# A two-pass attention backward kernel: first-pass steps re-ordered, one PSUM bank per head's softmax, slots for long VectorE work, output product per head

## Chip, cores, metric

One core of one Trainium2 chip. The metric is the device time of one execution in microseconds, as the median of several. Kernels that are compared ran on the same chip in alternating rounds; a ratio is the mean time of one kernel's fast runs over the mean of the other's fast runs of the same rounds, so it is not quite the ratio of the medians quoted beside it. A run over 1.5% above the fastest of its kernel counts as slow and stays out of the ratios. A verdict is "faster" or "slower" when the whole 95% interval of the ratio lies beyond 2%, "same" when it lies within 2%, and "unclear" when it reaches across that bound.

In the profile lines PE is TensorE (its matmuls), PEld its weight loads, DVE is VectorE, ACT ScalarE, POOL GpSimd, SP SyncE. The granted clock (PEclk) is the share of TensorE's full clock that the profile records. Stage figures come from the one profiled run of each kernel.

## The reference, cut to what matters

A transformer block in decode form (one query token, batch 2) and all its gradients:

```python
B, Sq, D = 2, 1, 640;  Hq = Hkv = 32;  Sk, Dh = 4096, 128;  Dff = 1728      # bf16
h  = x + softmax((LN(x) @ wq) . k_cache * Dh**-0.5) . v_cache @ wo
h2 = h + relu(LN(h) @ w1) @ w2
# outputs: h2 and the gradients of x, k_cache, v_cache, wq, wo, w1, w2 for a given grad_out
```

There are 64 (batch, head) pairs, each with 1 MB of K and 1 MB of V. K and V are read once in a first pass (scores, softmax, output and some sums), V once more in a second pass, and 2 MB of gradients are written per pair. The kernel moves 372.7 MB in all.

## The kernel before: the parts that matter

The first pass is a software pipeline over i: stage c works on head i (transposes of K, scores), p on head i-1 (softmax, P times K), r on head i-2 (sums over V). One generator yields after each step. In the iterations read in the timelines (kernel before, 77 to 85 us) PE and VectorE keep the order in which this code issues their instructions, apart from PE's weight loads, which run ahead of matmuls.

```python
def p1_iter(i, dve_group):
    ...
    # step 0: KT0 = transpose_group(K, 0)                       PE, copied out by ScalarE
    # step 1: u_half(0), KT1, mx_ps <- rmax, gmax, m_part(0)
    # step 2: scores 0, KT2, nb, ep = exp(...), u_half(1), m_part(1)
    # step 3: scores 1, KT3, m_part(2), pk_part(0)
    # step 4: scores 2, m_part(3), tot_ps, pk_part(1)
    # step 5: m_part(4), m_part(5); VectorE: tot, rtot, P_bf, pk_part(2)
    if c is not None:                                         # step 6
        matvec_group(c["s"], c.pop("KT3"), 3, q)
        rmax = small.tile([128, 1], BF16, tag="rmax", name="rmax")
        nc.vector.reduce_max(out=rmax[:], in_=c["s"][:], axis=AX.X)
        c["rmax"] = rmax
    if r is not None:
        m_part(6)
    if p is not None:
        pk_part(3)
    yield
    # step 7: m_part(7), MT and OU written by ScalarE
```

The attention output of all heads goes through wo in the middle of the run, after the first batch:

```python
def middle_gen(b):
    nc.vector.tensor_copy(out=OFc[:, :, b], in_=OU[:, b, :, 0])
    yield
    a_ps = pst([128, ND], FP32, "mid", "a_ps")
    for c in range(ND):
        for h in range(H):
            nc.tensor.matmul(a_ps[:, c:c + 1], lhsT=wo_t[:, h, c * 128:(c + 1) * 128], rhs=OFc[:, h, b:b + 1], ...)
            if h % (4 if b == 0 else 8) == 3:
                yield
    # norm, MLP forward and backward, then go_group: what the second pass needs
```

`middle_gen` is background work: a few of its yields run per step, by a credit (`RATES`). The second pass starts at i = 49, every second iteration, and runs alone from i = 66 on. The kernel divides PSUM (the memory that its matmuls write) into eight banks by tag, `PSB`; the tag "tiny" is one bank that all small softmax results shared.

## Time and profile before

| | before |
|---|---|
| median of 3 | 1045.98 us (1043.9 to 1046.0) |
| span of the profiled run | 1044.0 us |
| HBM traffic | 372.7 MB, mean 357 GB/s |
| heads 12, 31, 43, 46, 63 leave the first pass at | 116.3, 246.4, 338.8, 364.6, 530.4 us |

The clock hands of the last row are the copies MT, one per head, at the end of its first pass. From the profile's page, the busy share of PE and DMA and the granted clock in tenths, in 40 slices of 26.1 us:

```profile
PE   6999989999998988878895665547998987676795
PEclk9988999899969889887875575566555555667555
DMA  9999999999857578898999999999899998999697
```

To see: PE and DMA both near 90% in the first ten slices, DMA low in slices 11 to 15 (the middle), and PE near half clock in the second pass (0.59 and 0.57 in the two windows from 530 to 960 us), where DMA is full (0.98 and 0.97).

### The profile page before, as it was taken

What the parts mean: (1) busy time and instruction counts of PE and PEld (TensorE: products, weight loads), DVE (VectorE), ACT (ScalarE), POOL (GpSimd) and SP (SyncE); (2) the same over time, 40 slices, a digit from 0 to 9 for tenths busy, and PEclk for the clock granted to TensorE, in tenths of its full rate; (3) what the DMA queues carried; (4) which work ended last, traced back from release to release, by engine and by line L of the source; (5) the groups of instructions that cost most, each with busy time, mean ns of one, the idle gap of its engine ahead of it and who ended that gap; (6) DMA issues with size and microseconds to landing.
All of it is one profiled execution on the core that took longest, in us unless ns stands there. A gap on an engine that the chain in (4) does not pass through costs nothing.

```text
span 1044.0 us, 32292 instructions
## 1 busy us (share of the span) xinstructions
PE 843.8 (81%) x14111; PEld 730.7 (70%) x14111; DVE 698.8 (67%) x1654; ACT 644.8 (62%) x985; POOL 95.2 (9%) x216
## 2 busy tenths in 40 slices
PE   6999989999998988878895665547998987676795
PEld 5988888889987887778784554436675765665553
DVE  3656777766549777776665768777876755566465
ACT  4555555467766586667674564546777766555684
POOL 0000000000000000000011111111111111111121
PEclk9988999899969889887875575566555555667555
DMA  9999999999857578898999999999899998999697
GB/s 350 382 400 405 363 364 379 347 349 351 323 206 282 205 278 314 346 379 342 363 413 425 371 384 394 355 402 361 326 412 422 398 393 329 421 422 401 231 374 319
DMA packets 59758, 372.70 MB, mean 357 GB/s; under 512 B 5760, under 2 KB 15424, under 8 KB 17376
## 3 DMA queue, kind: packets, MB, share of 16 engines
q1 hardware_dynamic: 38960, 221.50, 56.2%
q0 software_dynamic: 20656, 149.14, 34.7%
q8 instruction: 110, 1.80, 0.7%
q14 instruction: 32, 0.26, 0.1%
HBM read 221.48 MB, written 149.13 MB: 355 GB/s over the span
## 4 chain that ended last, share of the span: by engine, by line
PE 40%; DMA 26%; DVE 16%; issue 10%; ACT 5%; POOL 1%; SPq 0%; POOLq 0%; ACTq 0%; DVEq 0%
PE t_ps L274 16%; DMA out_dram<-gV 15%; PE m_ps L304 9%; DMA Wt<-in_A_v_cache_dram 6%; DVE pk L310 5%; DVE gK L550 4%; PE o_ps L652 4%; PE m_ps L320 4%; PE s_ps L285 3%; DVE junk L436 3%; ACT t_sb L279 2%; DMA Vt<-in_A_v_cache_dram 2%; DMA Kt<-in_A_k_cache_dram 2%; PE dp_ps L285 1%; DVE gV L550 1%
## 5 line engine op out<-in xcount | busy, mean ns | idle before, releaser
L279 ACT COPY t_sb<-t_ps 128x1024 bf16<-128x1024 bf16 x489 | 490.4, 1013 | 190.4 <-PE t_ps L274 184.1
L274 PE MATMUL t_ps<-ident_bf,Wt 128*128 128x128 bf16 x2048 | 239.2, 289 | 16.6 <-DMA Wt<-in_A_v_cache_dram 15.3
L274 PEld LDWEIGHTS <-Wt 128*128 128x128 bf16 x2048 | 185.4, 132 | 67.7 <-issue 50.0
L285 PEld LDWEIGHTS <-t_sb 128*128 128x128 bf16 x4096 | 171.1, 104 | 67.4 <-ACT t_sb L279 58.5
L310 DVE TENSOR_TENSOR pk<-Kt,ep 128x1024 bf16<-128x1024 bf16 x256 | 174.5, 683 | 45.0 <-ACT ep L353 41.2
L550 DVE TENSOR_TENSOR gV<-rb,pp 128x2048 bf16<-128x2048 bf16 x128 | 155.8, 1217 | 66.8 <-DMA out_dram<-gK 31.7
L550 DVE TENSOR_TENSOR gK<-rb,gsp 128x2048 bf16<-128x2048 bf16 x128 | 153.6, 1218 | 59.5 <-DMA out_dram<-gV 59.5
L304 PE MATMUL m_ps<-pk,Vt 128*128 128x129 bf16 x2048 | 193.3, 234 | 0.0
L274 PE MATMUL t_ps<-ident_bf,Kt 128*128 128x128 bf16 x2048 | 172.9, 234 | 2.3 <-DMA Kt<-in_A_k_cache_dram 2.3
L304 PEld LDWEIGHTS <-Vt 128*128 128x128 bf16 x2048 | 135.8, 104 | 4.5
L274 PEld LDWEIGHTS <-Kt 128*128 128x128 bf16 x2048 | 132.4, 104 | 3.6 <-DMA Kt<-in_A_k_cache_dram 2.7
L285 PE MATMUL dp_ps<-goc,t_sb 128*128 128x1 bf16 x2048 | 97.6, 169 | 45.7 <-ACT t_sb L279 43.4
L594 POOL DMA_DIRECT2D out_dram<-gV x64 | 34.2, 534 | 667.7 <-DVE gV L550 638.1
L285 PE MATMUL s_ps<-qc,t_sb 128*128 128x1 bf16 x2048 | 89.3, 164 | 4.2 <-DVE gsp L585 2.0
L406 ACT ACTIVATE MT<-m_ps,rtot 128x128 bf16<-128x128 f32 x64 | 23.5, 368 | 105.3 <-PE m_ps L304 105.3
L320 PEld LDWEIGHTS <-Kt 128*128 128x128 bf16 x2048 | 64.7, 97 | 20.3 <-issue 18.9
L277 DVE COPY t_sb<-t_ps 128x1024 bf16<-128x1024 bf16 x43 | 29.7, 690 | 71.6 <-PE t_ps L274 71.5
L320 PE MATMUL m_ps<-ep,Kt 128*128 128x1 bf16 x2048 | 70.8, 164 | 7.6 <-ACT OU L407 6.3
L655 ACT CAST ot<-o_ps 128x512 bf16<-128x512 f32 (+3 forms) x120 | 59.8, 526 | 11.7 <-PE o_ps L652 10.4
L564 ACT CAST rb<-rb_ps 128x256 bf16<-128x256 f32 x64 | 24.4, 381 | 49.7 <-DVE gK L550 37.9
L610 POOL DMA_DIRECT2D out_dram<-gK x64 | 34.0, 531 | 226.8 <-DVE gK L550 183.7
L436 DVE CUSTOM_DVE_ANT_0 junk<-wo_t,hbc 128x640 bf16<-128x640 bf16 x64 | 52.1, 815 | 0.1
(168 smaller groups left out, 703.2 us busy)
## 6 DMA issues: line engine op xcount, KB each, us to landing
Kt<-in_A_k_cache_dram SPq DMA_DIRECT2D x64, 1024.0 KB, 8.0
Vt<-in_A_v_cache_dram SPq DMA_DIRECT2D x64, 1024.0 KB, 7.6
Wt<-in_A_v_cache_dram SPq DMA_DIRECT2D x64, 1024.0 KB, 10.6
out_dram<-gV POOLq DMA_DIRECT2D x64, 1024.0 KB, 8.2
out_dram<-gK POOLq DMA_DIRECT2D x64, 1024.0 KB, 9.3
wo_t<-in_A_wo_dram SPq DMA_DIRECT2D x4, 1280.0 KB, 9.5
wqs<-in_A_wq_dram SPq DMA_DIRECT2D x5, 1024.0 KB, 17.4
out_dram<-ot POOLq DMA_DIRECT2D x5, 1024.0 KB, 5.5
```

What stands on the lines that cost most here:

```text
L274: nc.tensor.transpose(t_ps[:, j, :], nat[:, g * GT + j, :], ident_bf[:])
L279: nc.scalar.copy(out=t_sb[:], in_=t_ps[:])
L285: nc.tensor.matmul(dst[:, sc:sc + 1], lhsT=t_sb[:, j, :], rhs=vec, start=True, stop=True)
L304: nc.tensor.matmul(r["m"][:, 0:129], lhsT=r["V"][:, sc, :], rhs=r["pk"][sc // GT][:, sc % GT, 0:129], start=False, stop=(sc == NSC - 1))
L310: nc.vector.tensor_tensor(out=pk[:, :, 0:128].rearrange("p s (a two) -> p s a two", two=2), in0=p["K"][:, sl, :].rearrange("p s (a two) -> ...
L320: nc.tensor.matmul(r["m"][:, 129:130], lhsT=r["K"][:, sc, :], rhs=r["ep"][:, sc, 0:1], start=(sc == 0), stop=False)
L436: nc.vector.tensor_tensor_reduce(out=junk[0:kc, 0:width], in0=in0, in1=in1, scale=1.0, scalar=0.0, op0=ALU.mult, op1=ALU.add, accum_out=acc)
L550: nc.vector.tensor_tensor(out=pairs_view(dst[:, sl, :]), in0=row.rearrange("p (a two) -> p a two", two=2)[:, None, :, :].to_broadcast([128 ...
L594: nc.gpsimd.dma_start(out=natural(out_3, b, h), in_=gV[:])
L610: nc.gpsimd.dma_start(out=natural(out_2, bp, hp), in_=gK[:])
L652: nc.tensor.matmul(o_ps[0:P, 0:nn], lhsT=L[:, bass.ds(c0 + k, P, step=cc)], rhs=R[:, n0:n0 + nn], start=True, stop=True)
L655: nc.scalar.copy(out=ot[0:P, k, n0:n0 + nn], in_=o_ps[0:P, 0:nn])
```

## The change

Its intent, as far as the code shows it: let nothing in the first pass wait for the shared scratch bank; put long VectorE reductions only where no engine waits behind them; take the two bursts of 160 wo products out of the middle, so that the second pass can begin three iterations earlier; spread the second pass's steps over the iteration, and load its V tile (W) one iteration earlier. The core of the diff (cuts marked):

```diff
-    PSB = {"tps": 2, "sps": 3, "m": 1, "tiny": 1, "mid": 1}
+    PSB = {"tps": 2, "sps": 3, "m": 1, "a": 1, "mid": 1}
@@ p1_iter: steps 0 to 4 re-ordered (KT0, KT1 together; both u halves together; nb, ep at step 3) ... @@
+            c["bank"] = pst([128, 512], FP32, "sps", "s_ps")     # mx, nb, tot in other columns of it
@@ step 5 @@
         if r is not None:
-            m_part(4)
             m_part(5)
+        if c is not None:
+            matvec_group(c["s"], c.pop("KT3"), 3, q)
+            rmax = small.tile([128, 1], BF16, tag="rmax", name="rmax")
+            nc.vector.reduce_max(out=rmax[:], in_=c["s"], axis=AX.X)
+            c["rmax"] = rmax
         if p is not None:
+            pk_part(2)
             tot = ...; rtot = ...; P_bf[...] = ...
-            pk_part(2)
@@ new @@
+    def a_head():
+        b, h = pairs[a_next[0]]
+        if h == 0:
+            a_bank[0] = pst([128, ND], FP32, "a", "a_ps")
+        nc.vector.tensor_copy(out=OFc[:, h, b:b + 1], in_=OU[:, b, h, 0:1])
+        for c in range(ND):
+            nc.tensor.matmul(a_bank[0][:, c:c + 1], lhsT=wo_t[:, h, ...], rhs=OFc[:, h, b:b + 1], ...)
+        a_next[0] += 1
+    def a_heads(i): ...            # up to two heads g <= i - 3
@@ slots @@
+    def turn():
+        while slot[0] <= 0:
+            yield 0.0
+        slot[0] -= 1
@@ go_group, gx2 and ga reductions @@
+            yield from turn()
@@ second pass: dp and row broadcasts in one bank, gK first, then transposes, gV last; 7 background
@@ steps per second-pass head where there were 5; steps placed by MIXED and REST in the mixed stage
-    M0_ITERS = 15
+    M0_ITERS = 12
+        ahead = plan[n + 1][1] if n + 1 < len(plan) and ii is not None else jj    # W queued earlier
@@ main loop @@
+        for k, _ in enumerate(p1_iter(i, i < H + 1)):
+            ...
+            if k == 5:
+                a_heads(i)
+            pump()
+            slot[0] = ...          # 1 or 2 at k = 1, 1 at k = 6, else 0
+            bg_step(0, rate)
```

Not shown: the weights are loaded in another order (the pieces of wo before w1), the credit of the background work is capped, MT has 50 buffers instead of 52, and the weight gradients' outputs rotate over three banks instead of two.

More of the change, by code (lines that the diff above doesn't have):

```diff
@@ L54 @@
     GH = 8
-    NMT = 52
+    NMT = 50
     def f_kc(c):
@@ L326, in p1_iter @@
             c["KT0"] = transpose_group(c["K"], 0)
+            c["KT1"] = transpose_group(c["K"], 1)
         yield
@@ L330, in p1_iter @@
             u_half(0)
-        if c is not None:
-            c["KT1"] = transpose_group(c["K"], 1)
+            u_half(1)
+            give(r["Kg"])
         if p is not None:
@@ L335, in p1_iter @@
             bhp = bp * H + hp
-            mx_ps = pst([1, 128], FP32, "tiny", "mx_ps")
-            nc.tensor.matmul(mx_ps[:], lhsT=p["rmax"][:], rhs=ident_bf[:], start=True, stop=True)
+            mx = p["bank"][0:1, 64:192]
+            nc.tensor.matmul(mx, lhsT=p["rmax"][:], rhs=ident_bf[:], start=True, stop=True)
             gmax = small.tile([1, 1], BF16, tag="gmax", name="gmax")
-            nc.vector.reduce_max(out=gmax[:], in_=mx_ps[:], axis=AX.X)
+            nc.vector.reduce_max(out=gmax[:], in_=mx, axis=AX.X)
         if r is not None:
@@ L343, in p1_iter @@
         if c is not None:
-            c["s"] = pst([128, NSC], FP32, "sps", "s_ps")
+            c["bank"] = pst([128, 512], FP32, "sps", "s_ps")
+            c["s"] = c["bank"][:, 0:NSC]
             matvec_group(c["s"], c.pop("KT0"), 0, q)
             c["KT2"] = transpose_group(c["K"], 2)
+        if r is not None:
+            m_part(1)
+        yield
+        if c is not None:
+            matvec_group(c["s"], c.pop("KT1"), 1, q)
         if p is not None:
-            nb_ps = pst([128, 1], FP32, "tiny", "nb_ps")
-            nc.tensor.matmul(nb_ps[:], lhsT=ones_bf[0:1, :], rhs=gmax[:], start=True, stop=True)
+            nbp = p["bank"][:, 200:201]
+            nc.tensor.matmul(nbp, lhsT=ones_bf[0:1, :], rhs=gmax[:], start=True, stop=True)
             nb = small.tile([128, 1], FP32, tag="nb", name="nb")
-            nc.scalar.mul(out=nb[:], in_=nb_ps[:], mul=-SCALE)
+            nc.scalar.mul(out=nb[:], in_=nbp, mul=-SCALE)
             ep = small.tile([128, NSC, 2], BF16, tag="ep", name="ep")
@@ L356, in p1_iter @@
         if r is not None:
-            u_half(1)
-            give(r["Kg"])
-            m_part(1)
+            m_part(2)
+        if c is not None:
+            c["KT3"] = transpose_group(c["K"], 3, dve_group)
         yield
-        if c is not None:
-            matvec_group(c["s"], c.pop("KT1"), 1, q)
-            c["KT3"] = transpose_group(c["K"], 3, dve_group)
-        if r is not None:
-            m_part(2)
         if p is not None:
             pk_part(0)
-        yield
+            pk_part(1)
+        if r is not None:
+            m_part(3)
         if c is not None:
@@ L371, in p1_iter @@
         if r is not None:
-            m_part(3)
+            m_part(4)
         if p is not None:
-            tot_ps = pst([128, NSC], FP32, "tiny", "tot_ps")
-            nc.tensor.matmul(tot_ps[:], lhsT=ones_bf[:], rhs=ep[:, :, 0], start=True, stop=True)
-            pk_part(1)
+            totp = p["bank"][:, 256:256 + NSC]
+            nc.tensor.matmul(totp, lhsT=ones_bf[:], rhs=ep[:, :, 0], start=True, stop=True)
         yield
         if r is not None:
-            m_part(4)
             m_part(5)
+        if c is not None:
+            matvec_group(c["s"], c.pop("KT3"), 3, q)
+            rmax = small.tile([128, 1], BF16, tag="rmax", name="rmax")
+            nc.vector.reduce_max(out=rmax[:], in_=c["s"], axis=AX.X)
+            c["rmax"] = rmax
         if p is not None:
+            pk_part(2)
             tot = small.tile([128, 1], FP32, tag="tot", name="tot")
-            nc.vector.reduce_sum(out=tot[:], in_=tot_ps[:], axis=AX.X)
+            nc.vector.reduce_sum(out=tot[:], in_=totp, axis=AX.X)
             rtot = small.tile([128, 1], FP32, tag="rtot", name="rtot")
@@ L388, in p1_iter @@
             p["rtot"] = rtot
-            pk_part(2)
         yield
-        if c is not None:
-            matvec_group(c["s"], c.pop("KT3"), 3, q)
-            rmax = small.tile([128, 1], BF16, tag="rmax", name="rmax")
-            nc.vector.reduce_max(out=rmax[:], in_=c["s"][:], axis=AX.X)
-            c["rmax"] = rmax
         if r is not None:
@@ L410, in p1_iter, with a_heads @@
         yield
+    a_next = [0]
+    a_bank = [None]
+    def a_head():
[4 more added lines that the diff above has]
+        for c in range(ND):
+            nc.tensor.matmul(a_bank[0][:, c:c + 1], lhsT=wo_t[:, h, c * 128:(c + 1) * 128], rhs=OFc[:, h, b:b + 1],
+                             start=(h == 0 and c == 0), stop=(h == H - 1 and c == ND - 1))
+        a_next[0] += 1
+    def a_heads(i):
+        for _ in range(2):
+            g = a_next[0]
+            if g > i - 3 or g >= NP1:
+                return
+            b, h = pairs[g]
+            if b == 0 and i < W_AT[1 + h * 4 // H] + 4 or b > 0 and ("a", b - 1) not in done:
+                return
+            a_head()
     def bcast_cols(colsrc, n, kc_of, dst):
@@ L437, in ttr @@
                                        op0=ALU.mult, op1=ALU.add, accum_out=acc)
+    slot = [99]
+    def turn():
+        while slot[0] <= 0:
+            yield 0.0
+        slot[0] -= 1
     def one(src, b):
@@ L467, in middle_gen @@
     def middle_gen(b):
-        nc.vector.tensor_copy(out=OFc[:, :, b], in_=OU[:, b, :, 0])
-        yield
-        a_ps = pst([128, ND], FP32, "mid", "a_ps")
-        for c in range(ND):
-            for h in range(H):
-                nc.tensor.matmul(a_ps[:, c:c + 1], lhsT=wo_t[:, h, c * 128:(c + 1) * 128], rhs=OFc[:, h, b:b + 1],
-                                 start=(h == 0), stop=(h == H - 1))
-                if h % (4 if b == 0 else 8) == 3:
-                    yield
+        while a_next[0] < (b + 1) * H:
+            a_head()
+            yield
+        a_ps = a_bank[0]
         at_bf = small.tile([128, ND], BF16, tag="at_bf", bufs=1, name="at_bf")
@@ L481, in middle_gen @@
         nc.vector.tensor_copy(out=h32[:, 0, :], in_=h1c[:, :, b])
-        yield
+        yield ("a", b)
         yield from ln_fwd(h32[:], 1, x2c[:, :, b:b + 1], rstd2[:, b:b + 1])
@@ L507, in middle_gen @@
             for k in range(3):
+                yield from turn()
                 ttr(w1_t[:, c, k * FW:(k + 1) * FW], fbc[:, k * FW:(k + 1) * FW], gx2p[:, c, k:k + 1], FW)
@@ L540, in ga_gen @@
                 kc = f_kc(c)
+                yield from turn()
                 ttr(w2_t[0:kc, c, :], gbc[0:kc, :], ga[0:kc, b, c:c + 1], D, kc)
@@ L553, in outer_half @@
             in1=colp[:, sl, None, :].to_broadcast([128, HALF, 64, 2]), op=ALU.mult)
-    def p2_rows(j):
-        b, h = pairs[j]
-        rb_ps = pst([128, 256], FP32, "tiny", "rb_ps")
-        nc.tensor.matmul(rb_ps[:, 0:128], lhsT=goc[:, h, b:b + 1].to_broadcast([128, 128]), rhs=ident_bf[:],
-                         start=True, stop=True)
-        nc.tensor.matmul(rb_ps[:, 128:256], lhsT=qsc[:, h, b:b + 1].to_broadcast([128, 128]), rhs=ident_bf[:],
-                         start=True, stop=True)
-        rb = mats.tile([128, 256], BF16, tag="rb", bufs=3, name="rb")
-        nc.scalar.copy(out=rb[:], in_=rb_ps[:])
-        pp = small.tile([128, NSC, 2], BF16, tag="pp", name="pp")
-        nc.gpsimd.tensor_copy(out=pp[:], in_=P_bf[:, b * H + h, :, None].to_broadcast([128, NSC, 2]))
-        S2.setdefault(j, {}).update(rb=rb, pp=pp)
     def p2_iter(j):
@@ L572, in p2_iter @@
         p = S2[j - 1] if j - 1 in S2 else None
-        if c is not None:
-            b, h = pairs[j]
-            go = goc[:, h, b:b + 1]
-            if "rb" not in c:
-                p2_rows(j)
-            c["T0"] = transpose_group(c["W"], 0)
-            gV = take("g", [128, NSC, 128], "gV")
-            outer_half(gV, c["rb"][:, 0:128], c["pp"], 0)
         if p is not None:
@@ L587, in p2_iter @@
                 in1=P_bf[:, bp * H + hp, :, None].to_broadcast([128, NSC, 2]), op0=ALU.add, op1=ALU.mult)
-        yield
         if c is not None:
-            c["dp"] = pst([128, NSC], FP32, "sps", "dp_ps")
-            c["T1"] = transpose_group(c["W"], 1)
-            matvec_group(c["dp"], c.pop("T0"), 0, go)
-            outer_half(gV, c["rb"][:, 0:128], c["pp"], 1)
-            nc.gpsimd.dma_start(out=natural(out_3, b, h), in_=gV[:])
-            give("g")
-        yield
-        if c is not None:
-            c["T2"] = transpose_group(c["W"], 2)
-            matvec_group(c["dp"], c.pop("T1"), 1, go)
+            b, h = pairs[j]
+            go = goc[:, h, b:b + 1]
+            bank = pst([128, 512], FP32, "sps", "dp_ps")
+            for k, col in enumerate((goc, qsc)):
+                nc.tensor.matmul(bank[:, 128 + k * 128:256 + k * 128],
+                                 lhsT=col[:, h, b:b + 1].to_broadcast([128, 128]), rhs=ident_bf[:],
+                                 start=True, stop=True)
+            c["dp"] = bank[:, 0:NSC]
+            rb = mats.tile([128, 256], BF16, tag="rb", bufs=3, name="rb")
+            nc.scalar.copy(out=rb[:], in_=bank[:, 128:384])
+            pp = small.tile([128, NSC, 2], BF16, tag="pp", name="pp")
+            nc.gpsimd.tensor_copy(out=pp[:], in_=P_bf[:, b * H + h, :, None].to_broadcast([128, NSC, 2]))
+            c.update(rb=rb, pp=pp)
+            c["T0"] = transpose_group(c["W"], 0)
         if p is not None:
@@ L603, in p2_iter @@
         yield
-        if c is not None:
-            c["T3"] = transpose_group(c["W"], 3)
-            give(c["Wg"])
-            matvec_group(c["dp"], c.pop("T2"), 2, go)
         if p is not None:
@@ L613, in p2_iter @@
         yield
-        if j + 1 < NP1 and ("go", (j + 1) // H, ((j + 1) % H) // GH) in done:
-            p2_rows(j + 1)
+        if c is None:
+            return
+        c["T1"] = transpose_group(c["W"], 1)
+        matvec_group(c["dp"], c.pop("T0"), 0, go)
+        yield
+        c["T2"] = transpose_group(c["W"], 2)
+        matvec_group(c["dp"], c.pop("T1"), 1, go)
+        yield
+        c["T3"] = transpose_group(c["W"], 3)
+        give(c["Wg"])
+        matvec_group(c["dp"], c.pop("T2"), 2, go)
+        gV = take("g", [128, NSC, 128], "gV")
+        outer_half(gV, c["rb"][:, 0:128], c["pp"], 0)
+        yield
+        outer_half(gV, c["rb"][:, 0:128], c["pp"], 1)
+        nc.gpsimd.dma_start(out=natural(out_3, b, h), in_=gV[:])
+        give("g")
         yield
@@ L650, in outer_rows @@
                     fw[0] += 1
-                    o_ps = pst([128, 512], FP32, "mid" if fw[0] % 2 else "m", "o_ps")
+                    o_ps = pst([128, 512], FP32, ("mid", "m", "a")[fw[0] % 3], "o_ps")
                     nc.tensor.matmul(o_ps[0:P, 0:nn], lhsT=L[:, bass.ds(c0 + k, P, step=cc)], rhs=R[:, n0:n0 + nn],
@@ L733, in bg_step @@
         q = (bg, bg2)[k]
-        credit[k] = credit[k] + rate if q else 0.0
+        credit[k] = min(credit[k] + rate, 2.0) if q else 0.0
         while q and credit[k] > 0.0:
-            credit[k] -= bg_one(q)
+            took = bg_one(q)
+            credit[k] -= took
+            if took == 0.0:
+                break
     def bg_until(mark):
+        slot[0] = 99
         while mark not in done:
             assert bg_one(bg) > 0.0, mark
-    M0_ITERS = 15
+    M0_ITERS = 12
     P2_AT = H + 2 + M0_ITERS
@@ L764 @@
                 queue.append(("K", ii))
-        if jj is not None and jj < NP1:
-            queue.append(("W", jj))
+        ahead = plan[n + 1][1] if n + 1 < len(plan) and ii is not None else jj
+        if ahead is not None and ahead < NP1 and ("W", ahead) not in queue:
+            queue.append(("W", ahead))
         if ii is not None and 1 <= ii <= NP1:
@@ L769 @@
         if ii in W_AT:
-            queue.append(("w", (5, 4, 0, 1, 2, 3)[W_AT.index(ii)]))
+            queue.append(("w", (5, 0, 1, 2, 3, 4)[W_AT.index(ii)]))
     queue.insert(0, ("wq", 0))
@@ L793, with p2_step @@
     fin = None
-    for n, (i, j) in enumerate(plan):
-        gens = []
-        if i is not None:
-            if i % QP == 0 and 1 <= i // QP < NQ:
-                q_piece(i // QP)
-                pump()
-            gens.append(p1_iter(i, i < H + 1))
+    g2 = None
+    MIXED = {1: 2, 3: 1, 4: 1, 6: 1}
+    REST = {1: 1}
+    def p2_step():
+        nonlocal g2
+        try:
+            next(g2)
+        except StopIteration:
+            g2 = None
+    for n, (i, j) in enumerate(plan):
+        if i is not None and i % QP == 0 and 1 <= i // QP < NQ:
+            q_piece(i // QP)
+            pump()
         if n + 3 < len(plan) and plan[n + 3][1] is not None:
@@ L803 @@
         if j is not None:
+            while g2 is not None:
+                p2_step()
             if j < NP1:
                 bg_until(("go", j // H, (j % H) // GH))
-            gens.append(p2_iter(j))
+            g2 = p2_iter(j)
         if i is None and j >= H - 1:
@@ L814 @@
             bg.append(("ga", ga_gen()))
-        rate = RATES[0 if i is not None and i <= H + 1 else 1 if j is None else 2 if i is not None else
-                     3 if j <= H else 4]
-        while gens:
-            for g in list(gens):
-                try:
-                    next(g)
-                except StopIteration:
-                    gens.remove(g)
-                    continue
+        rate = RATES[0 if i is not None and i <= H + 1 else 1 if j is None and i < P2_AT else
+                     2 if i is not None else 3 if j <= H else 4]
+        if i is None:
+            slot[0] = 99
+            while g2 is not None:
+                p2_step()
                 pump()
@@ L826 @@
                 bg_step(1, RATE2)
+            continue
+        at = MIXED if j is not None else REST
+        for k, _ in enumerate(p1_iter(i, i < H + 1)):
+            for _ in range(at.get(k, 0)):
+                if g2 is not None:
+                    p2_step()
+            if k == 5:
+                a_heads(i)
+            pump()
+            slot[0] = ((2 if rate == RATES[1] else 1) if k == 1 else 1 if k == 6 else 0) if i < P2_AT else int(k == 6)
+            bg_step(0, rate)
+            bg_step(1, RATE2)
         if i is not None and i in (H + 1, NP1 + 1):
```

## The prediction

> **What bounds the kernel now.** I read the page's busy shares and 40 slices first, then one window per stage, then one first-pass iteration in the timeline, then the waits of the mixed stage.
>
> No engine is the bound over the whole run, so the run has to be cut into stages. The scaled softmax rows (MT, one per head, written when a head leaves the first pass) are the clock hands: head 12 leaves at 116.3 us, head 31 at 246.4, head 46 at 364.6, head 63 at 530.4. The windows between them, with columns us, then busy us per engine, granted clock, DMA share and GB/s:
>
> ```profile
> core 0: us, PE busy (x) PEld busy (x) DVE busy (x) ACT busy (x) POOL busy (x), PEclk, DMA share, GB/s
> 116.00:246.00 130.00, 118.67 (x2567) 109.35 (x2565) 97.39 (x321) 75.31 (x136) 0.00 (x0) 0.97 0.96 359
> 246.00:365.00 119.00, 110.55 (x2312) 102.67 (x2310) 79.68 (x290) 79.31 (x131) 0.00 (x0) 0.88 0.74 266
> 365.00:530.00 165.00, 139.62 (x2708) 129.72 (x2706) 119.92 (x316) 113.04 (x172) 11.05 (x24) 0.87 0.88 340
> 530.00:706.00 176.00, 103.14 (x1656) 91.88 (x1653) 121.07 (x186) 92.41 (x114) 27.36 (x62) 0.59 0.98 391
> 706.00:960.00 254.00, 208.29 (x2390) 163.37 (x2391) 168.93 (x258) 173.48 (x257) 42.05 (x94) 0.57 0.97 389
> 960.00:1044.00 84.00, 62.28 (x562) 40.29 (x560) 46.76 (x60) 51.40 (x76) 12.86 (x28) 0.50 0.77 311
> ```
>
> To see: from 530 on the DMA engines are 97 to 98% busy at about 390 GB/s, so the second pass alone is bound by transfers. Up to 246 PE (91% busy) and DMA (96%) run close together. From 246 to 365, where the output projection, norms and MLP are threaded in, DMA falls to 266 GB/s and PE sets the pace. From 365 to 530 (both passes mixed) PE is 85% busy and DMA 88%.
>
> How tight PE is in a smooth first-pass iteration (6.17 us, heads 5 to 9) is seen at the end of one:
>
> ```profile
> 78.23 0.34 PE L285 MATMUL s_ps<-qc,t_sb 128*128 128x1 bf16 x8
> 78.41 0.47 PEld L304 LDWEIGHTS <-Vt 128*128 128x128 bf16 x8
> 78.43 0.63 PE L304 MATMUL m_ps<-pk,Vt 128*128 128x129 bf16 x8
> ```
>
> PE goes from the last score group (78.23) to the next product 0.20 us later. By such start-to-start pitches: transposes 4 x 0.55, score groups 4 x 0.2, column sums 0.8, m products 1.9, three small ones 0.3, together 6.0 us of the 6.17. Thus any wait put on PE's path is added almost whole.
>
> In the mixed stage a pair of iterations (one with, one without a second-pass head) takes 19.8 to 22.2 us by the same hands; the late load of W costs some 2 to 3 us of it:
>
> ```profile
> PE t_ps L274 <- DMA Wt<-in_A_v_cache_dram: 6.3, 3, 2.5
> ```
>
> [...] every iteration keeps the order of the source. So a matmul that waits for VectorE holds all PE work behind it. [...] (clock 0.50 at 290 to 300 us, where the norm's chain stalls PE; 1.00 at 130 to 140 us, where PE was 83% busy with short gaps). [...] here the uses inside the shared bank follow one another by data anyway, so I expect no new wait from that in the first pass.
>
> **Part by part.**
>
> *One bank per head's softmax, both column-sum halves together, transposes 0 and 1 together.* Removes the shared one-buffer scratch bank and small waits at the iteration's head: ScalarE's OU copy (0.16 us), rmax (0.15 to 0.2). K's buffer is released about 0.8 us earlier. Gain about 0.2 us of 6.17: base 6.0. In the mixed stage the three banks rotate over dp, s, s: the next dp always takes the previous dp's bank, so PE must wait for gsp between the last score group and the row broadcast: about 0.35 + 0.28 + 0.1 = 0.75 us per pair, new.
>
> *VectorE slots.* The long multiply-reduces (0.75 to 0.82 us; 28 for `ga`, 23 before the second pass can start) move to where nothing waits. Before, iterations with them ran at 6.6 to 7.4 us (heads 13 to 18) against 6.17. Gain up to 0.7 us each over about 15 iterations, some 8 us, if nothing else takes it.
>
> *wo product per head.* Takes two bursts of 160 products away (PE 16.9 us busy in all; the first, 8 us, lies on PE's path around 250 to 286, the second in the DMA-bound part). But each head's five products are issued at step 5, just after the last score group, and they read OFc, a VectorE copy queued **behind** rmax, pk part 2, tot, rtot and P_bf of the same step. rmax itself needs that score group. Pitches of those on VectorE from the timeline: rmax 0.10, pk 0.61 + 0.07, tot 0.22, rtot 0.19, P_bf 0.15, then the copy about 0.15, plus about 0.15 for the score group's own drain beyond its 0.20 pitch and the semaphores: **1.65 us in which PE waits**, where it now needs no wait at all. In the kernel before the same wait exists once, when a whole OFc is copied:
>
> ```profile
> who waited for it (us, times):
>   PE a_ps L473: 1.4, 1
> ```
>
> That is this wait's size by itself. With the products (5 x 0.045 to 0.05 = 0.25 us) an iteration becomes 6.0 + 1.65 + 0.25 = 7.9 us. It holds from i = 15 (with one exception, i = 19, where no head is due) to i = 65, since heads of the second batch start at i = 35, one per iteration.
>
> *Second pass three iterations earlier (12 for 15), W loaded one iteration earlier, its steps spread.* One more second-pass head lies in the mixed stage: 10 for 9; one fewer in the tail, 8 us. The middle fits: about 27 short steps (3.4 iterations), 15 reduces at three per iteration (5), 1 for the norm backward, 8 more reduces (2.7): 12 to 12.4 iterations.
>
> **The sum** (first-pass index i; head i-2 leaves at its end):
> - to the start of i = 15: 116.3 before, DMA-bound at over 400 GB/s in much of it; after 114.
> - i = 15 to 33: before 130 us. After 18 x 7.9 + 6.0 = 148.
> - i = 34 to 45: after 12 x 7.9 + 8 for the norm's stalls (in the kernel before, heads 38 and 39 took 11.3 each) = 103. Second pass starts at 365; before at 364.6, but then three heads further on.
> - mixed: work per pair 2 x 6.25 + 3.3 (32 transposes 2.2, scores 0.8, rows 0.3) = 15.8, at a clock near 0.9 17.5 us; waits 2 x 1.65 + 0.75 + about 0.5 for ScalarE copies = 4.5; 22 us. DMA would need 7.34 MB at 390 GB/s = 18.8, so PE binds. Ten pairs, the last without loads of K: 217. First pass ends at 582 (before 530).
> - tail: before 514; one head fewer, 8; some 10 from three banks for the weight gradients' outputs (their stretch 960 to 1044 runs at 311 GB/s) and more background steps per head: 496.
> Total 1078 span, about 1080 measured.
>
> **Rivals.**
> *A: the wait is hidden.* If PE would have waited there anyway (for DMA or ScalarE), the 1.65 us vanish. Then first pass to i = 33 in 240, 12 iterations at 6.7 plus 8, mixed pairs at the DMA's 19.3, tail 496: 240 + 88 + 191 + 496 = 1015 to 1030. For it: VectorE is free enough, W's wait goes, DMA sits at 0.74 in the middle. Against: PE's 97% in smooth iterations, and DMA demand at 7.9 us is only about 2.55 MB / 7.9 = 323 GB/s, so no transfer wait covers it. I give 0.25.
> *B: the wait is there in the first pass but the transfers pay it back*: loads run ahead and the DMA-bound tail takes less. The buffers (7 + 3 of 1 MB) hold at most about 10 MB, some 25 us, and they are full in the middle already. It would give 1045 to 1060. I give 0.25.
> *C: the wait is there in full, and the new banks or gsp wait cool PE's clock in the mixed stage*: 1080 to 1095. The full-wait case with C together 0.5.
>
> **Range and chances.** Weighting 1080 (0.5), 1055 (0.25) and 1025 (0.25) gives about 1060 in the mean, with the bulk above; I say 1066, 8 in 10 between 1018 and 1092. Over 2% slower means above 1067: 0.49. Over 2% faster means below 1025: 0.17. Between: 0.34.
>
> **What would show it.** Right: a wait of PE's a_ps products for VectorE's OFc of 1.4 to 1.8 us, about 50 times, 70 to 90 us in all; MT spacing near 7.9 us from head 13 to 43, where DMA share falls to 0.85; head 63 leaving near 580; W's wait gone. Wrong: OFc waits under 0.5 us each, or spacing under 7 us at DMA share over 0.95 (rival A), or a tail shorter than 480 us (B).

Its sum: 114 + 148 + 103 + 217 + 496 = 1078 us. What it says of the clock at 290 to 300 us misreads the trace and is corrected in the point-by-point part.

## The result, and the profile after

The changed kernel takes 1157.42 us in the median (1146.69 to 1164.6, 4 runs, the longest of them slow), before 1045.99 (4 runs, the fourth at 1056.22); the ratio of the fast runs is 1.101 (95% interval 1.0889 to 1.1131). It is 10% slower: the direction of the prediction, outside its range.

The same three lines of the page, slices now of 28.8 us:

```profile
PE   6998887777888788777877675567698976679763
PEclk8999687777777657988787756556555556855555
DMA  9999787756646436898898999899899989959998
```

The first four slices are close to those before. From the fifth on, about i = 15, clock and DMA fall and stay low until the second pass. By stage, from the stage windows of the changed kernel, cut at its own hands (heads 12, 31, 43, 63):

```profile
core 0: us, PE busy (x) PEld busy (x) DVE busy (x) ACT busy (x) POOL busy (x), PEclk, DMA share, GB/s
108.00:297.00 189.00, 147.37 (x2712) 142.95 (x2710) 103.75 (x361) 74.25 (x135) 0.00 (x0) 0.77 0.71 264
297.00:429.00 132.00, 108.88 (x1813) 103.64 (x1811) 68.65 (x255) 63.66 (x106) 0.00 (x0) 0.68 0.51 185
429.00:643.00 214.00, 174.84 (x3276) 165.50 (x3274) 135.21 (x365) 128.10 (x202) 12.72 (x29) 0.82 0.85 319
643.00:1152.00 509.00, 365.19 (x4378) 288.00 (x4374) 340.13 (x512) 315.84 (x441) 91.37 (x179) 0.56 0.93 369
```

Who waited for the tile OFc in the changed kernel (us in all, times):

```profile
  PE a_ps L426: 90.1, 48
```

And one iteration's end in its timeline (start, duration, engine, line; the bracket is the engine's idle time before):

```profile
221.46 0.69 DVE L277 COPY t_sb<-t_ps 128x1024 bf16<-128x1024 bf16 x1 [1.27 <-PE t_ps L274]
222.07 0.68 DVE L310 TENSOR_TENSOR pk<-Kt,ep 128x1024 bf16<-128x1024 bf16 x1
222.21 0.35 PE L285 MATMUL s_ps<-qc,t_sb 128*128 128x1 bf16 x8
222.74 0.69 DVE L310 TENSOR_TENSOR pk<-Kt,ep 128x1024 bf16<-128x1024 bf16 x1
...
223.41 0.19 DVE L387 TENSOR_REDUCE rmax<-s_ps 128x1 bf16<-128x32 f32 x1
223.51 0.69 DVE L310 TENSOR_TENSOR pk<-Kt,ep 128x1024 bf16<-128x1024 bf16 x1
...
224.60 0.24 DVE L395 TENSOR_SCALAR P_bf<-ep,rtot 128x32 bf16<-128x32 bf16 x1
224.75 0.21 DVE L423 CAST OFc<-OU 128x1 bf16<-128x1 f32 x2
...
224.96 0.39 PE L426 MATMUL a_ps<-OFc,wo_t 128*128 128x1 bf16 x10 [2.40 <-DVE OFc L423]
```

To see: PE's last score group ends at 222.56. VectorE is then still at pk parts 0 and 1 of the same head; rmax starts only at 223.41, and OFc comes behind pk part 2, tot, rtot and P_bf. PE stands still for 2.40 us. In the first batch VectorE also copies one of the four transposed groups out of PSUM, just ahead of this (L277, 0.69 us). In the second batch ScalarE makes that copy, and each wait is 1.6 us. That the copy makes the difference fits its length, but was not tested. The waits in heads 31 to 43:

```profile
PE a_ps L426 <- DVE OFc L423: 17.6, 11, 1.6
```

What the wait of 2.40 us does to the clock shows in two windows of its iteration, ahead of the wait's end and behind it:

```profile
218.00:225.00 7.00, 4.60 (x111) 4.39 (x109) 4.49 (x17) 2.67 (x5) 0.00 (x0) 0.94 0.95 377
225.00:230.00 5.00, 5.00 (x87) 4.87 (x87) 1.66 (x5) 2.45 (x4) 0.00 (x0) 0.57 1.02 408
```

After the wait PE is busy all the time, at a granted clock of 0.57. In heads 12 to 31 of this trace the clock records are 1.0 or 0.5 in turn, and the 15 stretches at 0.5 lasted 3.41, 6.83 or 10.24 us.

### The profile page after: what moved, and what is told of

It reads as the page before. It is cut to its first block, busy times and chain, and to the rows that moved or that the text cites. A ratio compares the mean times of both kernels' runs of the same rounds, so it can differ in the third digit from the quotient of the medians.

```text
span 1152.5 us, 32309 instructions
## 1 busy us (share of the span) xinstructions
PE 889.6 (77%) x14111; PEld 788.5 (68%) x14111; DVE 712.0 (62%) x1716; ACT 641.1 (56%) x985; POOL 106.0 (9%) x216
## 4 chain that ended last, share of the span: by engine, by line
PE 48%; DVE 18%; DMA 16%; ACT 10%; issue 7%; POOL 0%; SPq 0%; ACTq 0%; DVEq 0%; POOLq 0%
PE t_ps L274 20%; PE m_ps L304 11%; DMA out_dram<-gK 8%; ACT t_sb L279 7%; DVE pk L310 6%; PE m_ps L320 4%; PE o_ps L680 3%; DMA out_dram<-gV 3%; DVE gV L585 3%; PE s_ps L285 3%; DMA out_dram<-ot 2%; DVE gK L585 2%; PE dp_ps L285 2%; DMA Kt<-in_A_k_cache_dram 2%; PE a_ps L426 1%
## 5 line engine op out<-in xcount | busy, mean ns | idle before, releaser
L279 ACT COPY t_sb<-t_ps 128x1024 bf16<-128x1024 bf16 x489 | 483.0, 1016 | 207.5 <-PE t_ps L274 203.3
L274 PE MATMUL t_ps<-ident_bf,Wt 128*128 128x128 bf16 x2048 | 231.1, 286 | 1.9 <-ACT t_sb L279 1.0
L304 PE MATMUL m_ps<-pk,Vt 128*128 128x129 bf16 x2048 | 223.4, 249 | 0.6 <-issue 0.6
L274 PE MATMUL t_ps<-ident_bf,Kt 128*128 128x128 bf16 x2048 | 199.7, 264 | 5.2 <-issue 2.1
L274 PEld LDWEIGHTS <-Kt 128*128 128x128 bf16 x2048 | 166.7, 121 | 7.7 <-issue 5.6
L304 PEld LDWEIGHTS <-Vt 128*128 128x128 bf16 x2048 | 150.1, 110 | 8.1 <-issue 1.6
L277 DVE COPY t_sb<-t_ps 128x1024 bf16<-128x1024 bf16 x43 | 29.7, 691 | 93.0 <-PE t_ps L274 90.4
L341 DVE TENSOR_REDUCE gmax<-s_ps 1x1 bf16<-1x128 f32 x64 | 17.9, 280 | 109.6 <-PE s_ps L339 109.6
L426 PE MATMUL a_ps<-OFc,wo_t 128*128 128x1 bf16 x320 | 15.3, 164 | 90.1 <-DVE OFc L423 90.1
L426 PEld LDWEIGHTS <-wo_t 128*128 128x128 bf16 x320 | 15.6, 98 | 93.4 <-issue 93.3
L320 PE MATMUL m_ps<-ep,Kt 128*128 128x1 bf16 x2048 | 63.7, 165 | 1.7 <-ACT OU L410 1.7
L320 PEld LDWEIGHTS <-Kt 128*128 128x128 bf16 x2048 | 63.4, 102 | 1.9 <-issue 1.4
```

The lines of the kernel that those rows point to most:

```text
L274: nc.tensor.transpose(t_ps[:, j, :], nat[:, g * GT + j, :], ident_bf[:])
L277: nc.vector.tensor_copy(out=t_sb[:], in_=t_ps[:])
L279: nc.scalar.copy(out=t_sb[:], in_=t_ps[:])
L304: nc.tensor.matmul(r["m"][:, 0:129], lhsT=r["V"][:, sc, :], rhs=r["pk"][sc // GT][:, sc % GT, 0:129], start=False, stop=(sc == NSC - 1))
L320: nc.tensor.matmul(r["m"][:, 129:130], lhsT=r["K"][:, sc, :], rhs=r["ep"][:, sc, 0:1], start=(sc == 0), stop=False)
L426: nc.tensor.matmul(a_bank[0][:, c:c + 1], lhsT=wo_t[:, h, c * 128:(c + 1) * 128], rhs=OFc[:, h, b:b + 1], start=(h == 0 and c == 0), stop= ...
```

## The experiments

Twelve kernels ran, and all gave the reference's results. The theory (W, not to be mixed up with the tile W): PE's wait for OFc, and the clock that it costs, make the whole loss. The rival (R): the new order, bank or slots cost the time, and the wait is only where it shows.

### Move the wait away: copies one half iteration earlier

```diff
-        nc.vector.tensor_copy(out=OFc[:, h, b:b + 1], in_=OU[:, b, h, 0:1])      # in a_head, step 5
+            if k == 1:
+                a_copy(i)          # the same copies, issued behind gmax at step 1
             if k == 5:
                 a_heads(i)         # the products stay here
```

> The changed kernel, with only VectorE's copies of OFc issued at step 1 of the same iteration, behind gmax; the five products per head stay at step 5. Theory W (PE waits about 2.3 us per iteration for OFc, and that gap also lowers the granted clock): the wait falls from 90 us in all to under 10, heads 13 to 31 leave every 6.2 to 6.8 us instead of 10.0, clock there 0.95 or more instead of 0.76, and the whole run takes 1015 to 1045 us. Rival R (the re-ordered steps, the shared bank or the slots themselves cost the time, and the wait is only where it shows): the idle time moves to another place and the run stays over 1110 us.

Measured: 1049.35 us (1044.02 to 1052.01) beside 1048.69 for the kernel before; ratio 0.9999 (0.9958 to 1.0039). The wait and the first two stages:

```profile
  PE a_ps L427: 3.6, 2
```
```profile
108.00:237.00 129.00, 119.69 (x2720) 114.97 (x2718) 100.92 (x357) 73.83 (x136) 0.00 (x0) 0.97 1.00 386
237.00:337.00 100.00, 90.20 (x1819) 85.51 (x1817) 68.90 (x263) 62.19 (x105) 0.00 (x0) 0.85 0.68 245
```

The wait is gone, the clock is back at 0.97, heads 12 to 31 leave every 6.80 us instead of 9.98, and DMA is full (1.00). Moving 62 tiny copies took the whole 10% back. R falls. The time is just over what I expected (1015 to 1045): the rest of the change brings nothing in sum. That is taken up below.

### Undo the product per head

The wo product back in `middle_gen`, with 15 iterations before the second pass; all else as changed.

```diff
-            if k == 5:
-                a_heads(i)
+        # middle_gen: one OFc copy, then 160 products with yields, as in the kernel before
-    M0_ITERS = 12
+    M0_ITERS = 15
```

> The changed kernel with the wo product back in the middle (one copy and bursts of products as before, in bank a) and the second pass started after 15 iterations as before; all else as changed. Theory W: no OFc wait, heads 13 to 31 every 6.2 to 6.8 us, the middle about as long as before, 1020 to 1050 us. Rival R: over 1110 us, since order, bank and slots are still the new ones.

Measured: 1046.9 us (1043.33 to 1051.29), ratio 0.9984 (0.9937 to 1.003). Heads 12 to 31 every 6.45 us, clock 0.97. So order, bank and slots do not make the loss: the per-head product, in its place, was the part that cost 10%. (This edit also moves the start of the second pass back; the early copies did without that.)

### Keep PE busy during the wait

```diff
             if k == 5:
+                if 15 <= i <= H + 1:
+                    f_ps = pst([128, 128], FP32, "mid", "f_ps")
+                    for _ in range(30):
+                        nc.tensor.matmul(f_ps[:], lhsT=ones_bf[:], rhs=ident_bf[:], start=True, stop=True)
                 a_heads(i)
```

> The changed kernel with 30 matmuls that nobody reads (128 columns each, about 2 us at full clock) in front of the per-head products, in iterations 15 to 33 only: PE has more to do, but does not idle while it waits for OFc. If the gap lowers the clock (theory W, second half): clock in heads 13 to 31 from 0.76 to 0.95 or more, their spacing from 10.0 to 8.2 to 8.8 us, the run 20 to 35 us shorter than the changed kernel (about 1125). If the low clock has another cause: the extra work is added, spacing 11 to 12 us, run over 1175.

The 2 us in it are an estimate: in the kernel before eight transposes of 128 columns take PE 0.54 us at a clock of 1.00 (81.30 to 81.84 us), so 30 such matmuls about 2.0.

Measured: 1126.11 us (1122.25 to 1130.32), ratio 1.0738 to the kernel before, against 1.101 for the changed kernel (in other rounds). Heads 12 to 31 in 161.9 us instead of 189.5, 8.52 us each, although PE does 30 useless matmuls more per iteration:

```profile
109.00:271.00 162.00, 149.90 (x3294) 144.70 (x3292) 104.32 (x362) 73.61 (x136) 0.00 (x0) 1.00 0.83 306
```

The clock is 1.00 throughout; 0.7 us of the wait is left in an ordinary iteration. More work made the stretch 15% shorter. From head 31 on, where no fill runs, the same kernel has its waits of 1.6 us and a clock of 0.71 again (heads 31 to 43). So in these heads the idle time is what lowered the clock (0.77 with it, 1.00 with the fill in its place), and the loss has two parts: the wait, and the slow PE after it. The second part is 27.6 us of these 189.5 (189.5 to 161.9). PE's busy time says the same: 147.37 us in the changed kernel, 119.69 with the early copies, for nearly as many matmuls (2712 and 2720).

### The wait alone, in the kernel before

```diff
             c["rmax"] = rmax
+        if p is not None:
+            pk_part(3)                     # moved ahead of m_part(6) in the source
+        if c is not None and i >= 15:
+            dum = small.tile([128, 1], BF16, tag="dum", name="dum")
+            nc.vector.tensor_copy(out=dum[:], in_=rmax[:])
+            w_ps = pst([128, 1], FP32, "tiny", "w_ps")
+            nc.tensor.matmul(w_ps[:], lhsT=ones_bf[:], rhs=dum[:], start=True, stop=True)
         if r is not None:
             m_part(6)
```

> The kernel before, with one thing added from iteration 15 on: a copy of one column on VectorE behind rmax and pk part 3, and one small matmul of PE that reads it, in front of m parts 6 and 7 (so a wait of some 1.2 to 2 us and no other part of the change). Theory W: heads 13 to 31 from 6.85 us to 8.3 to 9.5 us each, clock under 0.9 there, the run 1110 to 1150 us. Rival R (the wait alone is absorbed in the old order): under 1065 us.

Measured: 1192.76 us (1185.98 to 1193.47), ratio 1.1353. Who waited for that copy, and the stretch of heads 12 to 31:

```profile
  DVE dum L401: 104.1, 48
```
```profile
115.00:323.00 208.00, 153.96 (x2587) 143.36 (x2585) 102.34 (x347) 76.87 (x138) 0.00 (x0) 0.72 0.65 231
```

One copy of one column and one matmul per iteration, with nothing else of the change, slow the old kernel by 13.5%, more than the 1110 to 1150 us that I expected. The waits are longer than I meant (2.0 to 3.6 us in heads 12 to 31, 104 us in all), since VectorE's queue was longer there than I had counted; the slowdown is larger accordingly.

### Half the wait

```diff
-            if k == 1:
-                a_copy(i)
             c["rmax"] = rmax
+        a_copy(i)                  # step 5, behind rmax, ahead of pk part 2, tot, rtot, P_bf
```

> The changed kernel with the copies of OFc between rmax and pk part 2 in the same step, so PE's wait is about 1.1 us in place of 2.4. If the clock falls only with gaps of about 2 us: clock in heads 13 to 31 at 0.93 or more, spacing 7.0 to 7.4 us, the run 1070 to 1090 us. If any such gap lowers it: clock under 0.85, spacing over 8 us, the run over 1105.

Measured: 1069.3 us (1066.45 to 1071.81), ratio 1.0163 (1.0106 to 1.022, unclear by the 2% rule). The waits (30.3 us in all) and the stretch of heads 12 to 31:

```profile
  DVE OFc L440: 30.3, 47
```
```profile
108.00:249.00 141.00, 120.20 (x2724) 115.81 (x2722) 102.86 (x358) 73.71 (x136) 0.00 (x0) 0.98 0.93 351
```

Waits of 1.15 us leave the clock at 0.98: heads leave every 7.42 us, within 0.3 of the sum of an undisturbed iteration (5.74), the products (0.25) and the wait (1.15). Only one of 16 such waits has a half-clock stretch at its end (131 us; a q projection followed there). In the changed kernel 16 of the 18 waits of 1.6 to 2.4 us in heads 12 to 31 bring one. In heads 31 to 43, where the wait is 1.6 us, eight of 11 are followed by one within 1.2 us. The step from the short waits to the long ones costs 88 us (1069 to 1157, in different rounds) and not only the 56 us by which the waits grow (90.1 against 30.3, plus 3.6 behind two late copies).

The length of a gap does not settle it alone. In the kernel before, a wait of 0.77 us (up to 202.25) was followed by half clock at 203.94, others of 0.77 us (up to 132.09 and 166.61) were not within 20 us, and one of 1.35 us (up to 287.38) was followed by 17 us of half clock from 289.28. What else counts was not tested.

### Where the rest of the change's gain went

With the early copies the changed kernel ends level with the kernel before, although head 31 leaves 9 us earlier (237.5 against 246.4). Three parts were undone one by one, all on the early-copy kernel and on one chip. The early-copy kernel itself ran on another chip, so they are compared with it through the ratio to the kernel before. By the 2% rule all three are unclear; their intervals exclude 1.

**W in its own iteration again:** `ahead = jj`.

> The early-copy kernel with W queued in its own iteration as before the change. If the earlier W only pushes K back in the same queue (K's wait of 15.6 us in the mixed stage stands where W's 15.3 us stood before): the waits change places again and the run stays within 1 per cent of the early-copy kernel. If W ahead is a real gain: 10 to 20 us longer.

Measured: 1035.44 us (1031.58 to 1036.09), ratio 0.983 (0.9765 to 0.9894) to the kernel before, where the early-copy kernel had 0.9999. Neither expectation came true: W ahead was not neutral and not a gain, it was a loss of 1.7%. PE's DMA waits in the mixed stage, early-copy kernel first, then with W in its own iteration:

```profile
PE t_ps L274 <- DMA Kt<-in_A_k_cache_dram: 15.6, 6, 4.8
```
```profile
PE t_ps L274 <- DMA Wt<-in_A_v_cache_dram: 3.6, 3, 1.4
PE t_ps L274 <- DMA Kt<-in_A_k_cache_dram: 2.4, 5, 0.7
```

In the kernel before, PE had waited 15.3 us for W over its mixed stage. Loading W an iteration ahead turned that into as much waiting for K, which shares the queue and the seven buffers; W in its own turn is nearly in time here. PE's DMA waits fall by 9.6 us; the mixed stage (heads 43 to 63) falls by 18 (199.2 to 181.3), and the rest of that I did not separate.

**Background steps of the second pass:** the new loop takes seven per head for five, so the weight gradients are done in fewer heads.

```diff
-    RATES = (0.2, 0.5, 0.15, 0.46, 0.3)
-    RATE2 = 0.9
+    RATES = (0.2, 0.5, 0.15, 0.33, 0.21)
+    RATE2 = 0.64
```

> The early-copy kernel with the background rates of the second pass times 5/7 (0.33, 0.21, 0.64), because the new loop takes seven background steps per second-pass head where the old one took five. Theory T (the weight-gradient work is now packed into fewer heads, makes PE the bound there at half clock and leaves the end idle of it): the stretch from head 63 of the first pass to the end falls from 512 us to 490 to 500, the run to 1025 to 1038. Rival: the new step order of the second pass costs the time, the run stays within 6 us of the early-copy kernel.

Measured: 1042.43 us, but 1027.72 to 1050.19 over four runs, of which the two longest count as slow; ratio 0.9831 (0.9723 to 0.9938), from two fast runs. In the profiled run, which is the fastest of the four, the time from head 63 to the end falls from 511.9 to 496.5 us. This one alone settles nothing. On top of the kernel with W in its own turn, the same rates give a stretch of 502.5 us against 511.5 (profiled runs).

**No slots:** `turn()` returns at once.

> The early-copy kernel without the slots (the long multiply-reduces go wherever the background credit puts them, as before). If the slots gain what they were made for: heads 13 to 31 from 6.5 to 7.0 us or more, and the run 8 to 20 us longer. If they only delay the middle: head 43 not later than with slots, the run the same within 6 us or shorter.

Measured: 1033.04 us (1027.62 to 1035.72), ratio 0.9813 (0.9752 to 0.9874). Heads 12 to 31 are no slower without slots (6.87 against 6.80 us), so the slots gain nothing where they were meant to. They do not delay the middle either: head 43 leaves at 341.1 us without them and 337.0 with them. The mixed stage, head 43 to 63, falls from 199.2 to 183.3 us. In it the early-copy kernel has this wait, and the one without slots has none of it in its list of waits:

```profile
PE d_ps L505 <- DVE pr L501: 7.0, 2, 3.5
```

Held back to one slot per iteration, the last reduction of a group of heads sits at the end of VectorE's queue, behind a 1.22 us product of the second pass, just ahead of matmuls that need it. That is 7 of the 16 us; where the other 9 went I did not separate.

**All three together, and three variants of that:**

> The early-copy kernel with all three undone that each cost something by itself: W queued in its own iteration, the second pass's background rates times 5/7, no slots. If the three act on different stages (mixed stage, tail, middle) their gains of 14 to 20 us each add for the most part: 1000 to 1015 us, 3 to 5 per cent faster than the kernel before. If they are the same gain counted three times (all of it ending in the transfer-bound second pass): 1028 to 1036 us.

> As the kernel with all three undone, but with the slots kept. If the slots cost time by themselves: 8 to 18 us longer than that one. If they don't: within 4 us of it.

> As the kernel with all three undone, and the second pass started after 10 iterations instead of 12, which the middle should just reach without the slots. If the time between heads 31 and the first store is transfer time lost: 4 to 10 us shorter than with 12. If the middle is not done by then and is drained at one go: the same or longer.

> The three undone as before, and the wo product in bursts in the middle with 15 iterations before the second pass, as in the kernel before: what is left of the change is the order, the bank and the second pass's steps. If the product per head (with its copy early) is worth something by itself: 8 to 18 us longer than the kernel with the product per head (1008). If the burst is hidden as well: within 5 us of it.

| kernel | median us | ratio to before (95%) |
|---|---|---|
| all three undone, copies early | 1008.39 | 0.9604 (0.9572 to 0.9637) |
| the same with slots | 1024.68 | 0.9760 (0.9717 to 0.9803) |
| the same without slots, second pass after 10 iterations | 1007.57 | 0.9597 (0.9564 to 0.9630) |
| all three undone, wo product in the middle, 15 iterations (other chip) | 1020.44 | 0.9744 (0.9706 to 0.9782) |

The three gains of 1.7 to 1.9% add up to about 4%, three quarters of their sum of 5.3%. The expectation had placed them in three different stages; the profiled runs show W's turn and the slots both in the mixed stage (199.2 us to 181.3 and 183.3 alone, 169.8 together with the rates) and the rates in the tail. Keeping the slots costs 16 us (1024.68 against 1008.39, same rounds). Starting after 10 instead of 12 iterations makes no difference (4 to 10 us less were expected, if the time before the first store is lost). The product per head, which cost 10% in its place, is worth 1.4% once its copy comes early, together with the start of the second pass three iterations earlier that it allows: the two were not separated, and the profiled runs show the gain in the tail (497.9 us against 518.9), not in the first pass (head 63 at 506.9 against 499.1). The stage windows of the kernel with all three undone (mixed stage and tail, cut at 340 and 520; head 63 leaves at 506.9):

```profile
340.00:520.00 180.00, 159.39 (x3340) 149.72 (x3338) 141.12 (x382) 132.98 (x208) 14.82 (x33) 0.92 0.99 396
520.00:1004.00 484.00, 363.64 (x4238) 288.14 (x4238) 324.17 (x479) 305.92 (x430) 83.73 (x175) 0.53 0.96 382
```

The mixed stage now runs with DMA at 0.99 and 396 GB/s, where the kernel before had 0.88 and 340 (365 to 530 us). The kernel as a whole is 4% faster than the kernel before.

## Why the prediction was right or wrong, point by point

| term of the sum | predicted us | measured us |
|---|---|---|
| to head 12 | 114 | 107.6 |
| heads 12 to 31 | 148 | 189.5 |
| heads 31 to 43 | 103 | 131.8 |
| mixed, heads 43 to 63 | 217 | 213.7 |
| head 63 to the end | 496 | 509.9 |

- **The wait's mechanism: right.** The OFc copy stands behind the rest of step 5 in VectorE's queue and holds PE. It occurs 48 times for 90 us (predicted about 50 times, 70 to 90 us). The early copies, and a like wait put into the old kernel, both show what it costs.
- **The failed step: the clock.** The prediction put a first-pass iteration at 6.0 + 1.65 + 0.25 = 7.9 us at full clock, that is, it added the wait at its own length and took from one window of the trace that short gaps leave the clock alone ("1.00 at 130 to 140 us, where PE was 83% busy with short gaps"). Those gaps were at most 0.8 us. The waits of 1.6 to 2.4 us brought the clock to 0.77 in heads 12 to 31 and 0.68 in the middle. That is about 28 of the 41 us missing in heads 12 to 31 (by the fill, and by PE's busy time) and about 19 of the 29 missing in the middle (PE busy 108.88 us against 90.20 with the early copies). Its other example was misread: at 290 to 300 us PE does not stall, it is busy all the time at half clock, and the norm's wait ahead of that lasted 1.35 us. So the trace before already had half clock behind a gap shorter than the 1.65 us that the prediction added:

```profile
287.38 0.38 PE L128 MATMUL csum<-ln_vs,ones_f 128*128 128x1 f32 x2 [1.35 <-DVE ln_vs L151]
290.00:300.00 10.00, 9.99 (x179) 9.23 (x176) 4.38 (x18) 6.70 (x12) 0.00 (x0) 0.50 0.48 160
```

- **The wait was undersized in the first batch:** 2.25 us in the mean over heads 12 to 31 instead of 1.65. The prediction started counting at rmax; in the trace VectorE is still 0.85 us away from it, at pk parts 0 and 1 (222.56 to 223.41), behind its copy of a transposed group. Over 18 iterations that is 11 us. Where VectorE has no such copy, from head 31 on, the wait is 1.6 us, as predicted. In the other direction the undisturbed iteration is 5.74 us and not 6.0.
- **The middle** missed by 29 us: 19 by the clock, as said. Most of the rest was there without the wait: rival A put 88 us for a middle without it, and the early-copy kernel takes 99.5.
- **The mixed stage** was right (22 us a pair predicted, 21.4 measured). PE's busy time came out as predicted (174.84 us for 10 x 17.5), and so, nearly, did OFc's wait (28.8 us in 18 times, for 33) and the end of W's wait. Two errors cancelled, which is luck: the clock was 0.82 and not 0.9, and the wait for gsp (0.75 us per pair) never showed.
- **The tail** was 14 us too short: it counted more background steps and a third bank as a gain. The steps were rather a loss: at 5/7 of the rate the stretch is 15 us shorter in one profiled pair and 9 in another. What the third bank did was not tested.
- **Rival A** (1015 to 1030 without the wait): the early-copy kernel shows what the change is without it, 1049 us. So the prediction also overrated the rest. **Rival B** had no support: the tail did not pay the lost time back. **Rival C**, a colder clock, was the right kind of effect in the wrong stage; I placed it in the mixed stage and gave it too little.
- **Readings that were too wide:** DMA at 97 to 98% "from 530 on" holds to 960 us only (0.77 and 311 GB/s after that, as the table shows), and the pairs of 19.8 to 22.2 us leave out the shorter ones at both ends of the mixed stage.

## What to carry to other kernels

When an instruction on a busy engine reads a result of another engine, count from what that engine still has in its queue at that moment, not only from the instructions of the same step (here the copy itself took 0.15 us, and PE waited 2.40 us for it at 224.96); and issue tiny producers (here a copy of one column) as early as their data allows. Here a regular PE wait cost more than its length, because it lowered the clock: 18 waits of 1.1 us in the mean left it at 0.98 and 18 of 2.25 us took it to 0.77; with useless matmuls in the wait's place it stayed at 1.00. A large re-ordering can hide several parts that each lose something: undo them one at a time on top of the mended kernel. Here the late copy, the early W, the slots and probably the background rate each lost something, and without them the change gains 4%.
